# Gated mix of a state-space convolution and a bilinear GLU on one core: first weights split by blocks, inverse sets joined, planner's durations replaced

## The chip, the cores and the metric

The program runs on one core of a Trainium2 chip. Its engines work side by side, each through a list of instructions of its own in a fixed order: TensorE (PE) multiplies matrices, VectorE (DVE) and ScalarE (ACT) do elementwise work, GpSimd (POOL) and SyncE (SP) here mostly issue DMAs. The metric is the device time of one execution in microseconds. Before the change the median of three runs is 632.51 us (631.53 to 634.56).

## The reference

With x = A_u (2048 tokens, 512 channels):

```python
g = sigmoid((x * gate_w).sum(-1, keepdims=True))
a = conv(x, K) + x * D_skip        # K[d,l] = 2 Re sum_n C dt exp(A dt l), N=128, by FFT of length 4096
b = ((B_x @ w_gate) * (B_x @ w_up)) @ w_down      # 512 -> 1792 -> 512
out = g * a + (1 - g) * b
```

All data are float32.

## The kernel before

**The GLU.** The 1792 hidden columns are 14 blocks f of 128, taken in five groups of 3, 2, 3, 3, 3 (`GROUPS`); the tokens are four chunks of 512. One step (`hidden`, 56 in all) is one f for one chunk: 4 gate products into `pg` and 4 up products into `pu`, one for each 128 rows kt of the inputs, then `h` = pg times pu. `down` multiplies h into `y`, 4 products for a step. Each product is three fp32r matmuls: operands are split into a high part (`xhi`, `whi`, `dhi`, `hh`: a ScalarE cast) and a low part (`xlo`, `wlo`, `dlo`, `hl`: a VectorE subtraction). ScalarE scales y into `acc`, which a DMA adds into the output in DRAM; of the last chunk of the last group VectorE sums y into `kt` instead (`ends`).

**The convolution.** For 16 blocks b of 32 channels VectorE and ScalarE build tables of powers (`phases`, `amplitudes`, `direct_powers`, `x_table`, `v_table`) and PE multiplies them into the filter (the set `k<-v,x`, `k_block`). For each quarter q of the channels there follow: the first transform of the filter (`k<-kt,w1k_t`), the second transform of filter and input for T = 0 to 3 (`k<-in,w2s`; of the last quarter `k<-v,w2s` and `k<-x,w2s`), the pointwise product (`m_product`, VectorE), the inverse (`k<-y,w3s`, `m_inverse`), and the last step (`k<-in,w_t` or `k<-v,w_t`, `m_last`), which is scaled by the gate into `ts` and added to the output by DMA. Nearly all these sets write the four PSUM banks `k` and take PE about 1 to 2 us each. The first transform of the input (`u_part`) is eight sets, `k<-in,w_t` too.

**What sets the order.** Each piece of work is a task with an engine, a duration in us, a rank and its inputs (`Work.add`). `Work.run` is a list scheduler: it always takes the task that can start first by its own clock (ties by rank), and writes the instructions of each engine in that order. A task's inputs count as there at the end of their tasks plus a lag (`LAG`); a step's gate and up products may not start before `after` = 10.3 us times the number of the step. On the chip nothing is rescheduled: each engine takes its list in order and waits where an input is late. Before any product PE runs a warm-up (`warm`): products of zeros into a scratch bank.

In the trace all instructions carry line 98 (a helper records them), so they are told apart by their tiles.

Of the kernel before, what the change touches and what calls it, by code (L numbers as in the profile page):

```python
# [45 lines left out]
def fourier_matrices():  # L46
# [17 lines left out]
    for k in range(64):  # L64
# [20 lines left out]
        w4[0], w4[1] = 1.0, (-1.0) ** n1  # L85
    parts = (w1, w1k, w2.reshape(P, 32, 64), w3.reshape(P, 8, 2, 2, 64), w4)
# [56 lines left out]
class Work:  # L143
# [8 lines left out]
    LAG = {"pe": 0.7}  # L152
# [33 lines left out]

    def inputs(self, task):

        lag = self.LAG.get(task.engine, 0.15)
        at = task.after  # L190
        for d in task.deps:
            if d.end is None:
                return None
            at = max(at, d.end + (lag if d.engine != task.engine else 0.0))
        return at

    def slots(self, task, at):

        lag = self.LAG.get(task.engine, 0.15)
        taken = {}  # L200
        for tile in task.tiles:
            if tile.made is not None:
                continue
            n = taken.get(tile.key, 0)
            taken[tile.key] = n + 1
            place = len(tile.had) + n
            if not tile.loose and tile.turn != place:
                return None
            if place >= tile.bufs:
                for d in tile.had[place - tile.bufs].users:  # L210
                    if d.end is None:
                        return None
                    at = max(at, d.end + (lag if d.engine != task.engine else 0.0))
        return at

    def run(self):
# [5 lines left out]
        while any(left.values()):  # L222
# [30 lines left out]
            free[t.engine] = t.end  # L253
# [15 lines left out]
def gated_mix_kernel(  # L269
# [118 lines left out]
    def first_loads():  # L388
# [3 lines left out]
        w0 = load_two(lambda k: ("w", 0, k), in_ev, None, False)  # L392
        x01 = load_two(lambda k: ("x", 0, k), in_y, None, False)
        for t, k, src in ((x01, 0, xsrc(0)), (w0, 0, wts[0][:, :D]), (w0, 1, wts[0][:, D : 2 * D]), (x01, 1, xsrc(1))):
            add("sp", 0.42, lambda t=t, k=k, src=src: sp.dma_start(t.t[:, k], src), w=[(t, k)], dma=256, rank=-1)
        x23 = xT[2 * P : 4 * P, :D].rearrange("(k p) t -> p k t", k=2)
        load_two(lambda k: ("x", 0, 2 + k), in_y, x23)
# [8 lines left out]
        def warm():  # L406
            for _ in range(3):
                pe.matmul(scratch.t, zero.t[:, :P], zero.t, start=True, stop=True)

        add("pe", 4.0, warm, r=[zero], w=[scratch], rank=-1)  # L410

    def weights(fs):
        for f in fs:
            ws[f] = [new("glu", n, [P, 2 * D], F32R, len(GROUPS[0])) for n in ("whi", "wlo")]
            for c in range(2):
                load(("w", f, c), wts[f][:, c * D : (c + 1) * D])
                split(ws[f][0], ws[f][1], c, ("w", f, c))
            if f == 0:
                for kt in range(1, KT):
                    tokens_first(0, kt)  # L420
# [26 lines left out]
    def product(pg, which, w, x, kt, after):  # L447
        base = which * D + kt * P

        def fn():  # L450
            for n, (a, b) in enumerate(THREE):
# [4 lines left out]
        add("pe", 0.69, fn, r=[(w[0], which), (w[1], which), x[0], x[1]], w=[pg], rank=2, after=after)  # L456
# [5 lines left out]
    def hidden(f):  # L462
# [3 lines left out]
        after = T_STEP * len(steps)  # L466
# [5 lines left out]
        for which, kt in pairs:  # L472
            product(pg[which], which, ws[f], x[kt], kt, after)
# [15 lines left out]
    def down(y, r, h, w, first, last):  # L489
# [6 lines left out]
        add("pe", 0.69, fn, r=[*h, *w], w=[y], rank=2)  # L496
# [22 lines left out]
    def ends():  # L519
# [7 lines left out]
        for r, y in ending:  # L527
            t = t0 + r
            add(
                "dve", 0.69,  # L530
# [4 lines left out]
            )  # L535
            add(
                "dve", 0.25,
                lambda r=r: dve.tensor_tensor(
                    out=sums.t[:, r, P * (KT - 1) :], in0=sums.t[:, r, P * (KT - 1) :], in1=late["fin"].t[:, r],
                    op=ALU.add,  # L540
                ),
                r=[late["fin"]], w=[(sums, r)], rank=0.5,
# [40 lines left out]
    def u_part(c):  # L583
# [28 lines left out]
        add("pe", 2.0, fn, r=[ut, m_w1], w=banks[0] + banks[1], rank=1, hold=sts)  # L612
# [130 lines left out]
    def amplitudes(bs):  # L743
# [6 lines left out]
        def exps():  # L750
            for k, l in enumerate(POWERS):
                act.activation(e.t[:, : TB * len(bs), k].rearrange("p (n d) -> p n d", d=TB), rates(), AF.Exp, scale=float(l))

        add("act", 1.3 + NP * (0.13 + 0.0021 * TB * len(bs)), exps, r=[par], w=[e])
# [3 lines left out]
    def phases(b):  # L758
# [12 lines left out]
        def sines():  # L771
            act.activation(rt.t, t.t, AF.Abs)
            act.activation(t.t, t.t, AF.Sin, scale=-TWO_PI)
            act.activation(rt.t, rt.t, AF.Sin, scale=-TWO_PI, bias=half_pi[:, 0:1])

        add("act", 3.6 if b % 2 or not b else 2.3, sines, r=[m_const], w=[t, rt])
# [20 lines left out]
    def leads(b):  # L797
# [4 lines left out]
        add("act", 0.42, lambda: act.copy(x.t[:, :, :, 0], C()), r=[par], w=[(x, ("l", 2))])  # L802
# [58 lines left out]
    def v_table(b):  # L861
# [8 lines left out]
        add("act", 1.3, copies, r=[ri], w=[(v, 2)])  # L870
# [5 lines left out]
        for to, of, n in ((32, 0, 16), (56, 32, 8)):  # L876
# [12 lines left out]
            add("act", 2 * us - 0.2, sq_act, r=src_parts, w=[(v, ("r", k)), sq])  # L889
# [12 lines left out]
    def k_block(b, x, v):  # L902
# [15 lines left out]
        add("pe", 2.07, kgen, r=[x, v], w=[pk], rank=0, hold=[kt])  # L918
# [10 lines left out]
    def k_first(q, kt):  # L929

        tt(0.19, lambda: kt.t[:, 48, :], lambda: kt.t[:, 48, :], lambda: skip[:, q], ALU.add, [m_skip], [kt])
        for h in range(2):
# [17 lines left out]
            add("pe", 2.1, fn, r=[kt, m_w1k], w=banks, rank=-1, hold=sts)  # L950
# [59 lines left out]
    def m_second(q, ins, w):  # L1010
# [18 lines left out]
        add("pe", 2.1, fn, r=[*ins, w], w=banks[0] + banks[1], rank=1, hold=tos)  # L1029
# [40 lines left out]
    def m_inverse(q, T, y, w):  # L1070

        banks, ts = [bank() for _ in range(4)], stage([P, 2, 4, P])

        def fn():
            for i in range(2):
                for k in range(2):
                    for e in range(2):
                        for j in range(4):
                            lanes, cs = slice(32 * j, 32 * j + 32), slice(P * i, P * i + P)
                            pe.matmul(  # L1080
                                banks[j].t[64 * e : 64 * e + 64, cs], w.t[lanes, i, e, k], y.t[lanes, k, e, cs],
                                start=k == 0, stop=k == 1, tile_position=(32 * j, 64 * e),
                            )

        add("pe", 1.15, fn, r=[y, w], w=banks, rank=1, hold=[ts])
        for j in range(4):
            evict(
                q, j, 0.4, lambda j=j: ts.t[:, :, j],
                lambda j=j: banks[j].t[:, : 2 * P].rearrange("p (i d) -> p i d", i=2), [banks[j]], [(ts, j)],
            )  # L1090
        add(
            "sp", 0.42,
            lambda: sp.dma_start(
                y_d[q, 32 * T : 32 * T + 32].rearrange("(j a) n d -> (a n) j d", j=8),
                ts.t.rearrange("p i j d -> p (i j) d"),
            ),
            r=[ts], w=[(m_y, (q, T))], dma=512,
        )


    def m_last(q, half):
# [31 lines left out]
        add("pe", 1.9, fn, r=src, w=banks, rank=1, hold=fins)  # L1133
        for i, f in enumerate(banks):
# [15 lines left out]
            args = ("dve", 0.69, mix_dve) if q == KT - 1 else ("act", 1.2, mix_act)  # L1150
# [13 lines left out]
    def transforms(q):  # L1164
# [11 lines left out]
        now = [loads(0)]  # L1176
        for T in range(4):
# [4 lines left out]
            m_inverse(q, T, m_product(T, k, u2), w3_s)  # L1182
# [88 lines left out]
```

## Time and profile before

| | before |
|---|---|
| median of 3 runs | 632.51 us |
| the profiled execution | 633.44 us |
| its span, first to last instruction | 631.7 us |
| PE busy | 612.6 us, 97% |
| VectorE busy | 495.4 us, 78% |
| ScalarE busy | 399.6 us, 63% |
| GpSimd busy | 106.1 us, 17% |

PE is busy nearly all the time, and the chain of waits that ended last runs over PE for 81% of the span. The first product starts at 7.68 us and the last one at 625.32 us; the span ends 6.3 us after that. VectorE's share falls late: in the page's 40 slices it is busy 5 to 9 tenths up to 520 us, and 1 to 6 tenths behind that.

### The profile page before, as it was taken

To read this page: it belongs to the slowest core of one execution; us is meant where nothing else is said; L and a number is where in the kernel's file an instruction comes from. 1 tells how busy PE (TensorE), PEld (TensorE's weight loads), DVE (VectorE), ACT (ScalarE), POOL (GpSimd) and SP (SyncE) were. 2 spreads that over 40 slices of the span, in tenths; PEclk is the share of its full clock that TensorE was granted. 3 is DMA by queue.
4 is the path that set the end of the run, shared out by engine and by line. 5 is a ranking of instruction groups with operands and counts; after the bars stand their busy time and mean duration, and the time that the engine had idled before them with its cause. 6 is when DMAs were issued, how large, how long until landed. Compare 5 with 4: busy or idle time off the path is not lost.

```text
span 631.7 us, 18000 instructions
## 1 busy us (share of the span) xinstructions
PE 612.6 (97%) x7526; PEld 468.8 (74%) x7526; DVE 495.4 (78%) x764; ACT 399.6 (63%) x931; POOL 106.1 (17%) x157
## 2 busy tenths in 40 slices
PE   8989999999999999999999999999999999998996
PEld 5667677678688887787778778768887887776783
DVE  6958999989969899799778898977998872146524
ACT  4477877885876795668687765785786543333320
POOL 3231523111021021002110202030101011130101
PEclk9999999999999999999999999999999999999998
DMA  8896949559779599578988959597979699897956
GB/s 309 295 335 248 328 136 369 178 159 287 190 183 300 148 242 274 136 217 190 260 196 199 292 159 247 156 190 190 276 165 265 184 255 252 285 248 206 239 129 116
DMA packets 111893, 142.64 MB, mean 226 GB/s; under 512 B 7876, under 2 KB 66756, under 8 KB 111556
## 3 DMA queue, kind: packets, MB, share of 16 engines
q1 hardware_dynamic: 90100, 105.05, 52.7%
q0 software_dynamic: 21568, 36.45, 28.0%
q8 instruction: 59, 0.97, 0.6%
q14 instruction: 22, 0.18, 0.1%
q10 hardware_dynamic: 144, 0.00, 0.0%
HBM read 81.96 MB, written 59.51 MB: 224 GB/s over the span
## 4 chain that ended last, share of the span: by engine, by line
PE 81%; issue 7%; DVE 5%; DMA 4%; POOL 1%; ACT 1%; POOLq 0%
PE y L98 22%; PE pg L98 20%; PE pu L98 20%; PE k L98 19%; DMA x_d<-xhi 2%; DVE x L98 2%; DMA su_d<-ts 1%; DVE v L98 1%; POOL x_d L98 1%; DMA y<-in_xT 1%; DVE m L98 1%; POOL su_d L98 0%; DVE hl L98 0%; DVE wlo L98 0%; DVE ri L98 0%
## 5 line engine op out<-in xcount | busy, mean ns | idle before, releaser
L98 POOL DMA_DIRECT2D out<-acc x60 | 51.5, 916 | 372.2 <-ACT acc L98 341.7
L98 PE MATMUL y<-dhi,hl 128*128 128x512 f32 x224 | 91.4, 408 | 3.8 <-DVE hl L98 3.5
L98 PE MATMUL pg<-xhi,wlo 128*128 128x512 f32 x224 | 90.3, 403 | 3.6 <-ACT h L98 1.5
L98 PE MATMUL pu<-xhi,wlo 128*128 128x512 f32 x224 | 89.7, 400 | 0.6 <-DVE h L98 0.6
L98 PE MATMUL pg<-xlo,whi 128*128 128x512 f32 x224 | 87.6, 391 | 0.1
L98 PE MATMUL y<-dlo,hh 128*128 128x512 f32 x224 | 87.5, 391 | 0.0
L98 PE MATMUL pg<-xhi,whi 128*128 128x512 f32 x224 | 87.5, 390 | 0.0
L98 PE MATMUL y<-dhi,hh 128*128 128x512 f32 x224 | 87.4, 390 | 0.0
L98 PE MATMUL pu<-xlo,whi 128*128 128x512 f32 x224 | 87.4, 390 | 0.0
L98 PE MATMUL pu<-xhi,whi 128*128 128x512 f32 x224 | 87.3, 390 | 0.0
L98 DVE TENSOR_TENSOR h<-pu,h 128x512 f32<-128x512 f32 x56 | 38.6, 689 | 55.9 <-PE pu L98 36.1
L98 ACT ACTIVATE acc<-y,ngate 128x512 f32<-128x512 f32 x76 | 51.5, 686 | 36.5 <-PE y L98 28.9
L98 ACT CAST hh<-h 128x512 fp32r<-128x512 f32 x56 | 34.7, 621 | 57.5 <-DVE h L98 57.5
L98 ACT COPY ts<-k 128x256 f32<-128x256 f32 (+1 forms) x144 | 51.2, 435 | 21.3 <-PE k L98 21.3
L98 PEld LDWEIGHTS y<-dhi,hl 128*128 128x128 f32 x224 | 42.0, 187 | 24.5 <-issue 7.9
L98 PEld LDWEIGHTS pg<-xhi,wlo 128*128 128x128 f32 x224 | 42.0, 187 | 21.0 <-issue 5.0
L98 ACT COPY h<-pg 128x512 f32<-128x512 f32 x56 | 32.9, 588 | 37.7 <-PE pg L98 25.3
L98 PEld LDWEIGHTS pu<-xhi,wlo 128*128 128x128 f32 x224 | 42.0, 188 | 14.8 <-issue 4.7
L98 PEld LDWEIGHTS y<-dhi,hh 128*128 128x128 f32 x224 | 42.1, 188 | 9.3
L98 PEld LDWEIGHTS pg<-xhi,whi 128*128 128x128 f32 x224 | 42.0, 188 | 9.1
L98 PEld LDWEIGHTS pu<-xhi,whi 128*128 128x128 f32 x224 | 42.1, 188 | 9.1
L98 PEld LDWEIGHTS pg<-xlo,whi 128*128 128x128 f32 x224 | 42.1, 188 | 8.6 <-DVE xlo L98 0.5
(105 smaller groups left out, 1128.6 us busy)
## 6 DMA issues: line engine op xcount, KB each, us to landing
out<-acc POOLq DMA_DIRECT2D x60, 256.0 KB, 6.3
xhi<-x_d SPq DMA_DIRECT2D x48, 256.0 KB, 5.1
xlo<-x_d SPq DMA_DIRECT2D x48, 256.0 KB, 5.2
raw<-in_wts SPq DMA_DIRECT2D x36, 256.0 KB, 4.6
su_d<-ts POOLq DMA_DIRECT2D x32, 256.0 KB, 6.2
sk_d<-ts SPq DMA_DIRECT2D x16, 512.0 KB, 5.7
y_d<-ts SPq DMA_DIRECT2D x16, 512.0 KB, 5.0
in<-sk_d SPq DMA_DIRECT2D x12, 512.0 KB, 7.4
```

The source lines that it names most:

```text
L98: got = getattr(self.engine, name)(*args, **kw)
```

## The change

1. The weights of the first block f = 0 are loaded in four pieces of 128 input rows (gate and up columns together, 128 KB each), the first by ScalarE's queue, the others by SP's between the tokens' loads; each piece is split by itself (`first_split`). In f = 0 of the first chunk the product of the two high parts comes first. The warm-up has two products instead of three.
2. `m_inverse` takes two T at once: one set of 64 matmuls instead of two of 32, four evictions of 512 columns instead of eight of 256, and rows of `w4` permuted to fit.
3. In `ends` VectorE adds `fin` before it adds y, so that y's sum is the last operation ahead of the output DMA.
4. The planner: other lags, an overlap between neighbouring tasks on ScalarE and VectorE, other durations; `after` 5 us earlier; the exponentials and the sines are three tasks each instead of one.

```diff
-    LAG = {"pe": 0.7}
+    LAG = {"pe": 0.06, "sp": 0.3, "pool": 0.3}
+    PE_LAG = 0.17
+    OVERLAP = {"act": 0.09, "dve": 0.08}
...
+    def ready(self, task, d):
+        if d.engine == task.engine == "pe":
+            return d.end
+        return d.end + self.LAG.get(task.engine, 0.03) + (self.PE_LAG if d.engine == "pe" else 0.0)
...
-            free[t.engine] = t.end
+            free[t.engine] = t.end - self.OVERLAP.get(t.engine, 0.0)
...
+        for kt in range(KT):
+            t, k, ks = xt[kt // 2], kt % 2, slice(P * kt, P * kt + P)
+            add("sp", 0.42, lambda t=t, k=k, kt=kt: sp.dma_start(t.t[:, k], xsrc(kt)), w=[(t, k)], dma=256, rank=-1)
+            e, q = ("sp", sp) if kt else ("act", act)
+            add(e, 0.42, lambda q=q, ks=ks: q.dma_start(w0.t[:, :, ks], wsrc[:, :, ks]), w=[(w0, ("k", kt))], dma=128, rank=-1)
...
-            for _ in range(3):
+            for _ in range(2):
                 pe.matmul(scratch.t, zero.t[:, :P], zero.t, start=True, stop=True)
...
+    def first_split(kt):
+        hi, lo, t, k = *ws[0], raws["w0"], ("k", kt)
+        cut = lambda x: x.rearrange("p (c d) -> p c d", c=2)[:, :, P * kt : P * kt + P]
+        src = lambda: t.t[:, :, P * kt : P * kt + P]
+        add("act", 0.38, lambda: act.copy(cut(hi.t), src()), r=[(t, k)], w=[(hi, k)], rank=0)
+        add("dve", 0.42, lambda: dve.tensor_tensor(out=cut(lo.t), in0=src(), in1=cut(hi.t).bitcast(F32), op=ALU.subtract),
...
+        three = THREE[::-1] if first else THREE
...
-        add("pe", 0.69, fn, r=[(w[0], which), (w[1], which), x[0], x[1]], w=[pg], rank=2, after=after)
+        add("pe", 0.681, fn, r=[(w[0], part), (w[1], part), x[0], x[1]], w=[pg], rank=2, after=after)
...
-        after = T_STEP * len(steps)
+        after = T_STEP * len(steps) - 5.0
...
-    def m_inverse(q, T, y, w):
-        banks, ts = [bank() for _ in range(4)], stage([P, 2, 4, P])
+    def m_inverse(q, T0, ys, ws):
+        banks, sts = [bank() for _ in range(4)], [stage([P, 2, 2, 2, P]) for _ in range(2)]
         def fn():
+            for t in range(2):
...
-        add("pe", 1.15, fn, r=[y, w], w=banks, rank=1, hold=[ts])
+        add("pe", 2.13, fn, r=[*ys, *ws], w=banks, rank=1, hold=sts)
...
-            m_inverse(q, T, m_product(T, k, u2), w3_s)
+            done.append((m_product(T, k, u2), w3_s))
+            if T % 2:
+                m_inverse(q, T - 1, *zip(*done))
+                done = []
```

**The order that comes of it.** VectorE at the start of the program (`small` is the chain for the time step, `xlo` and `wlo` the low parts of tokens and weights). Before:

```order
L98 TENSOR_SCALAR small<-small 128x4 x3
L98 SCALAR_TENSOR_TENSOR small<-small 128x4 x2
L98 TENSOR_SCALAR small<-small 128x4 x2
L98 TENSOR_TENSOR xlo<-y,xhi 128x512
L98 SCALAR_TENSOR_TENSOR small<-small 128x4 x2
L98 TENSOR_TENSOR wlo<-ev,whi 128x512
L98 SCALAR_TENSOR_TENSOR small<-small 128x4
L98 TENSOR_TENSOR wlo<-ev,whi 128x512
L98 SCALAR_TENSOR_TENSOR small<-small 128x4
L98 TENSOR_TENSOR xlo<-y,xhi 128x512
L98 SCALAR_TENSOR_TENSOR small<-small 128x4 x3
L98 TENSOR_TENSOR xlo<-y,xhi 128x512 x2
```

VectorE at the same place in the changed kernel:

```order
L100 TENSOR_SCALAR small<-small 128x4 x2
L100 TENSOR_TENSOR xlo<-y,xhi 128x512
L100 TENSOR_TENSOR wlo<-ev,whi 128x2x128
L100 TENSOR_SCALAR small<-small 128x4
L100 SCALAR_TENSOR_TENSOR small<-small 128x4 x2
L100 TENSOR_TENSOR xlo<-y,xhi 128x512
L100 TENSOR_TENSOR wlo<-ev,whi 128x2x128
L100 TENSOR_SCALAR small<-small 128x4 x2
L100 SCALAR_TENSOR_TENSOR small<-small 128x4
L100 TENSOR_TENSOR xlo<-y,xhi 128x512
L100 TENSOR_TENSOR wlo<-ev,whi 128x2x128
L100 SCALAR_TENSOR_TENSOR small<-small 128x4 x2
```

Before, both `wlo` of f = 0 stand ahead of the second `xlo`; now there are four half-size ones, one behind each `xlo`. A fourth `xlo` and `wlo` follow directly behind the rows shown.

TensorE around one inverse set (`k<-y,w3s`) between products of the GLU. Before:

```order
L98 MATMUL pu<-xhi,whi 128x512
L98 MATMUL k<-y,w3s 64x128 x32
L98 MATMUL pu<-xhi,wlo 128x512
L98 MATMUL pu<-xlo,whi 128x512
L98 MATMUL pu<-xhi,whi 128x512
```

TensorE around one inverse set in the changed kernel:

```order
L100 MATMUL pg<-xhi,whi 128x512
L100 MATMUL k<-y,w3s 64x128 x64
L100 MATMUL pg<-xhi,wlo 128x512
L100 MATMUL pg<-xlo,whi 128x512
L100 MATMUL pg<-xhi,whi 128x512
```

A set has 64 matmuls instead of 32, and there are 8 sets instead of 16. Counted over the whole list, the convolution's sets stand in 71 separate places between GLU matmuls before (the warm-up counted as one) and in 60 now. Between the first and the last of the sixteen sets `k<-v,x` stand 1428 of the 2016 GLU matmuls before and 1176 now; behind the set `k<-v,w_t`, the last of the convolution, 21 before and 243 now.

VectorE's last rows (`kt` is the sum of the last four row tiles, `ts` the convolution's part of it). Before:

```order
L98 SCALAR_TENSOR_TENSOR kt<-y,ngate,kt 128x512
L98 TENSOR_TENSOR ts<-k,gate 128x512 x3
L98 SCALAR_TENSOR_TENSOR kt<-y,ngate,kt 128x512
L98 TENSOR_TENSOR ts<-k,gate 128x512
L98 TENSOR_TENSOR kt<-kt,ts 128x128 x2
L98 SCALAR_TENSOR_TENSOR kt<-y,ngate,kt 128x512
L98 TENSOR_TENSOR kt<-kt,ts 128x128
L98 SCALAR_TENSOR_TENSOR kt<-y,ngate,kt 128x512
L98 TENSOR_TENSOR kt<-kt,ts 128x128
```

VectorE's last rows in the changed kernel:

```order
L100 TENSOR_TENSOR h<-pu,h 128x512
L100 TENSOR_TENSOR hl<-h,hh 128x512
L100 TENSOR_TENSOR h<-pu,h 128x512
L100 TENSOR_TENSOR hl<-h,hh 128x512
L100 SCALAR_TENSOR_TENSOR kt<-y,ngate,kt 128x512 x4
```

The four `ts<-k,gate` and the four `kt<-kt,ts` now stand together, before the last six pairs of `h` and `hl`, and the four sums over y close the list.

## Rows read from the trace of the kernel before

**Rows 1.** The page's first part: busy us, share of the span, instructions.

```profile
PE 612.6 (97%) x7526; PEld 468.8 (74%) x7526; DVE 495.4 (78%) x764; ACT 399.6 (63%) x931; POOL 106.1 (17%) x157
```

**Rows 2.** Stretches: us, busy of PE, PEld, DVE, ACT, POOL; clock; DMA.

```profile
83.44:520.48 437.04, 432.82 (x5909) 338.36 (x5908) 384.84 (x558) 313.10 (x735) 64.35 (x76) 1.00 0.79 214
62.00:120.00 58.00, 54.91 (x470) 39.58 (x468) 54.80 (x94) 46.02 (x99) 18.10 (x28) 1.00 0.72 254
```

**Rows 3.** PE's waits: who waited <- for whom: us, times, longest.

```profile
PE k L98 <- issue: 3.6, 4, 1.5
PE y L98 <- DVE hl L98: 3.5, 3, 1.5
PE pg L98 <- ACT h L98: 1.5, 2, 1.2
```

**Rows 4.** Timeline, 4 to 14 us: start, us, engine, operation.

```profile
4.96 0.58 DVE L98 TENSOR_SCALAR small<-small 128x4 f32<-128x4 f32 x3 [3.40 <-DMA small<-in_rows]
6.05 0.69 DVE L98 TENSOR_TENSOR xlo<-y,xhi 128x512 fp32r<-128x512 f32 x1
...
9.36 1.30 DVE L98 TENSOR_TENSOR xlo<-y,xhi 128x512 fp32r<-128x512 f32 x2
12.36 0.39 PE L98 MATMUL pg<-xhi,whi 128*128 128x512 f32 x1
12.89 0.58 ACT L98 COPY h<-pg 128x512 f32<-128x512 f32 x1
13.52 0.50 PE L98 MATMUL pg<-xhi,wlo 128*128 128x512 f32 x1
```

**Rows 5.** Groups by form: operation, count, busy us, mean ns, idle before.

```profile
L98 PEld LDWEIGHTS pg<-xhi,whi 128*128 128x128 f32 x224 | 42.0, 188 | 9.1
L98 PEld LDWEIGHTS k<-acc 128*128 128x128 f32 x6 | 1.9, 330 | 3.5 <-issue 2.1 <-DVE acc L98 1.5
```

**Rows 6.** Timeline of PE around one inverse set.

```profile
598.16 0.39 PE L98 MATMUL pg<-xlo,whi 128*128 128x512 f32 x1
598.39 0.39 PE L98 MATMUL pg<-xhi,whi 128*128 128x512 f32 x1
598.71 1.21 PE L98 MATMUL k<-y,w3s 32*64 32x128 f32 x64
599.85 0.50 PE L98 MATMUL pu<-xhi,wlo 128*128 128x512 f32 x1
600.18 0.40 PE L98 MATMUL pu<-xlo,whi 128*128 128x512 f32 x1
```

**Rows 7.** Timeline of PE: two halves of one set, back to back.

```profile
567.62 1.16 PE L98 MATMUL k<-v,w2s 64*32 64x128 f32 x64
568.51 1.16 PE L98 MATMUL k<-x,w2s 64*32 64x128 f32 x64
569.60 0.50 PE L98 MATMUL pu<-xhi,wlo 128*128 128x512 f32 x1
```

**Rows 8.** Groups by form, VectorE's two for a step, ScalarE's table loads.

```profile
L98 DVE TENSOR_TENSOR h<-pu,h 128x512 f32<-128x512 f32 x56 | 38.6, 689 | 55.9 <-PE pu L98 36.1 <-issue 16.7 <-ACT h L98 1.9
L98 DVE TENSOR_TENSOR hl<-h,hh 128x512 fp32r<-128x512 f32 x56 | 38.4, 685 | 8.6 <-ACT hh L98 8.6
L98 ACT ACT_TABLE_LOAD x20 | 25.7, 1283 | 2.8 <-DMA pb<-par_d 1.3 <-PEq L1260 1.2
```

**Rows 9.** Timeline of the end, PE and VectorE.

```profile
625.32 0.39 PE L98 MATMUL y<-dhi,hh 128*128 128x512 f32 x1
625.75 0.75 DVE L98 SCALAR_TENSOR_TENSOR kt<-y,ngate,kt 128x512 f32<-128x512 f32 x1 [0.96 <-PE y L98]
626.53 0.29 DVE L98 TENSOR_TENSOR kt<-kt,ts 128x128 f32<-128x128 f32 x1
```

**Rows 10.** DMA issues: queue, count, KB each, median us to landing.

```profile
out<-kt SPq DMA_DIRECT2D x4, 256.0 KB, 4.9
pb<-par_d SPq DMA_DIRECT2D x2, 32.0 KB, 2.7
```

More of the change, by code (lines that the diff above doesn't have):

```diff
@@ L212, in slots @@
                         return None
-                    at = max(at, d.end + (lag if d.engine != task.engine else 0.0))
+                    at = max(at, self.ready(task, d))
         return at
@@ L414, in weights @@
             ws[f] = [new("glu", n, [P, 2 * D], F32R, len(GROUPS[0])) for n in ("whi", "wlo")]
+            if f == 0:
+                for kt in range(KT):
+                    first_split(kt)
+                    if kt + 1 < KT:
+                        tokens_first(0, kt + 1)
+                continue
             for c in range(2):
@@ L445, in gated_mix_kernel, with product @@
     THREE = ((1, 0), (0, 1), (0, 0))
-    def product(pg, which, w, x, kt, after):
+    def product(pg, which, w, x, kt, after, first):
         base = which * D + kt * P
+        part = ("k", kt) if first else which
+        three = THREE[::-1] if first else THREE
         def fn():
-            for n, (a, b) in enumerate(THREE):
+            for n, (a, b) in enumerate(three):
                 pe.matmul(
@@ L472, in hidden @@
         for which, kt in pairs:
-            product(pg[which], which, ws[f], x[kt], kt, after)
+            product(pg[which], which, ws[f], x[kt], kt, after, not steps[1:] and f == 0)
         h = new("glu", "h", [P, D])
@@ L529, in ends @@
             add(
+                "dve", 0.25,
+                lambda r=r: dve.tensor_tensor(
+                    out=sums.t[:, r, P * (KT - 1) :], in0=sums.t[:, r, P * (KT - 1) :], in1=late["fin"].t[:, r],
+                    op=ALU.add,
+                ),
+                r=[late["fin"]], w=[(sums, r)], rank=0,
+            )
+            add(
                 "dve", 0.69,
@@ L534, in ends @@
                 r=[y, (m_gate, LAST)], w=[(sums, r)], rank=0,
[L535 to L542, printed above, removed]
             )
@@ L1101, in m_last @@
+        for h in range(2):
+            st = sts[h]
+            b0 = 32 * (T0 + h)
+            add(
+                "sp", 0.42,
+                lambda b0=b0, st=st: sp.dma_start(
+                    y_d[q, b0 : b0 + 32].rearrange("(u a) n d -> (a n) u d", u=8),
+                    st.t.rearrange("p t i j d -> p (t i j) d"),
+                ),
+                r=[st], w=[(m_y, (q, T0 + h))], dma=512,
+            )
     def m_last(q, half):
@@ L1174, in loads @@
             )
-        now = [loads(0)]
+        now, done = [loads(0)], []
         for T in range(4):
```

101 lines of the change are left out of this document (50 added, 51 removed).

## The prediction

> **What bounds the kernel now.** I read the page's busy shares first: PE 97%, VectorE 78%, ScalarE 63% [rows 1]. So PE's own list sets the time, and an edit counts by what it takes from PE's list, from PE's waits, or from the two ends where PE stands idle. Then the stretches: from the first table set `k<-v,x` (83.44 us) to the last (520.48 us) PE is busy 432.82 of 437.04 us, and VectorE 384.84 us [rows 2]. PE's waits for a named releaser are few: 3.5 us for `hl`, 1.5 us for the copy of `pg`, and 3.6 us of stops inside sets that have no releaser [rows 3]. Last the two ends: step 1 begins at 13.52 us [rows 4], and the last product starts at 625.32 us, 6.3 us before the span's end of 631.7 [rows 9].
>
> A GLU matmul takes 0.23 us from start to start (598.16 to 598.39, rows 6); over many, 0.227.
>
> **Joined inverse sets: -3.0 us.** A set runs from 598.71 to 599.85, 1.14 us. Going in costs 0.32 - 0.23 = 0.09 us, coming out 0.33 - 0.23 = 0.10 us [rows 6]. Two sets apart take 2 x 1.33 = 2.66 us. How long 64 matmuls take in one set no row shows for this shape. The nearest is the second transform, of which the first half takes 0.89 us up to the second's start and the second half 1.09 us up to the next product [rows 7]: a half that is followed by its like is shorter than one that is followed by something else. So a joined set takes 1.14 + 0.89 = 2.03 us at best, 2.28 us at worst, and 0.19 us around it. A pair saves 0.19 to 0.44 us, eight pairs 1.5 to 3.5 us. I take 3.0, near the row. The evictions fall from eight of 256 columns to four of 512 and lie on ScalarE, which is 63% busy. The joined set waits for the later of two products; the GLU matmuls behind it in PE's list would wait with it. That is inside the term for waits below. The writes to `y_d` stay sixteen of 512 KB, each half now up to one product later.
>
> **Fewer places between the products: -0.4 us.** The sets stand in 60 places instead of 71. Eight of the eleven come from the joining and are counted; the other three save at most 3 x 0.19 = 0.6 us and at least nothing.
>
> **The start: -0.4 us, from -1.5 to +2.6.** Before, `pg` of f = 0 gets its last product at 12.36 us, ScalarE copies it at 12.89, and the next step starts at 13.52, 1.16 us after that product [rows 4]. In the new order the high product is first, but the second and the third of each kt need `xlo` and `wlo`, so VectorE sets the pace. Its list up to the last `wlo` of f = 0 has four `xlo`, four half-size `wlo` and eight `small`. Before, four `xlo`, two whole `wlo` and seven `small` took from 6.05 to 9.36 + 1.30 = 10.66 us, 4.61 us [rows 4]. With 0.4 us for a half (an estimate between half of the 0.685 us of the same subtraction, rows 8, and the whole) and 0.1 for one more `small`, that is 4.9 us. The first `xlo` stands behind two `small`; their 2 KB are now issued second on ScalarE's queue, some 0.4 us later, so 4.96 + 0.4 + 0.4 = 5.8 us. The last low part is there at 10.7 us instead of feeding a product at 12.36; step 1 starts at 11.9 to 12.1: 1.5 us earlier at best. The same 1.5 MB are loaded as before, in smaller pieces; no row shows weights loaded so, and if a piece lands late the end of the range below covers it.
>
> [...]
>
> **The end: -0.7 us, from -2.5 to +0.3.** Behind the last product come a sum of 0.75 us, the addition of `ts` of 0.29 us [rows 9] and the output DMA. The addition now stands earlier: -0.29 us. The output DMAs took 4.9 us to land, in the company of GpSimd's last two additions of `ts` into the output; the smallest landing of the trace is 2.7 us for 32 KB [rows 10]. The last set of the convolution now has 243 GLU matmuls behind it instead of 21, 55 us instead of 5, so this company is gone: between 0 and -2.2 us, and I take -0.7. Against it: with two `y` buffers the third row tile's product waits for the first one's sum. From the start of a last product to its sum's end it takes 0.43 + 0.75 = 1.18 us [rows 9], and only four matmuls, 0.91 us, are there to cover it: +0.27. All of the last products stand behind that wait.
>
> **The planner: 0 us, from -5 to +20.** This moves nearly every row and adds no PE work. What it removes can be the waits for `hl` and `pg` [rows 3]. What it adds is pressure on VectorE. Between the first and the last `k<-v,x` there are 252 GLU matmuls fewer, 57.2 us, and by the order one second transform and one last set fewer (2 x 2.2 us by rows 7) and five joined inverse sets (5 x 2.28) for twelve (12 x 1.33): 9.0 us. So PE needs 437.0 - 57.2 - 9.0 = 370.8 us there, with its old waits. VectorE does 25 instructions fewer there (529 for 554), 23 of them on 128 x 512 at 0.687 us [rows 8]: it needs 384.8 - 15.8 = 369.0 us. That is a share of 99.5% where it had 88%; its best long stretch before was 54.80 of 58 us, 94.5% [rows 2]. What hides VectorE's waits before, its slack, is gone. In return the last 164 us are nearly free of it. I take 0: the waits that better durations remove against those that a full VectorE brings back.
>
> Two more table loads on ScalarE (22 for 20, 1.28 us each, rows 8) come from the split exponentials and sines; ScalarE's idle third hides them, and uncovered they cost 2.6 us. The read of the sums into `kt` now stands ahead of the last 14 loads of tokens on SP's queue; the first of them is needed over 100 matmuls, some 25 us, later, so I cost it at nothing. The host's permutation of `w4` costs nothing.
>
> **Sum.** -3.0 - 0.4 - 0.4 - 0.7 + 0 = -4.5 us. The profiled execution took 633.44 us, 0.93 more than the median of the runs: 633.4 - 4.5 = 628.9, as a median 628.0 us.
>
> **Rivals.** (A) VectorE becomes the bound of the table stretch. For it: 99.5%. Against: instructions interleaved by true durations leave fewer holes than the old order did. If it stays at 94.5%, its 369.0 us take 390.5, 19.7 more than PE's 370.8; 633.4 - 4.5 + 19.7 - 0.9 = 647.7 us. It decides from VectorE's waits of some 9 us in the stretch on: 1.8 are free, 4.5 eat the gains. (B) The planner also takes out PE's waits for `hl` and `pg`, 5.0 us: 623.0 us. For it: these are exactly waits that wrong lags make. Against: VectorE's fullness. [...] (D) The change doesn't give what it says: the joined sets wait for their second half and PE loses what it saved, leaving the ends: 631.4 us.
>
> **How the numbers follow.** My forecast, 628.0 with its own range of 624 to 632, has a chance of 0.37; A 0.21, B 0.20, C 0.12, D 0.10. About 0.5%, 3.2 us, can be told from no change. Faster by more (below 629.3): three quarters of mine, all of B, a little of C and D, 0.51. Slower by more (above 635.7): nearly all of A, 0.20. The rest, 0.29, is no change. The range goes to the better end of B, 619, and into A as far as 641, leaving out A's upper half.
>
> **What would show it.** Sets `k<-y,w3s` of 128 records (the trace counts two for each matmul of the order) and 2.0 to 2.3 us, eight of them. [...] From the last product to the span's end 5.4 us. Between the first and last `k<-v,x` about 371 us; 380 and more, with PE's waits for VectorE grown, is A. I am wrong if PE's waits for VectorE and ScalarE together pass 10 us, or fall under 1.

## The result, and the profile after

The changed kernel takes 637.13 us (median of 20 runs, 633.19 to 643.60) beside 633.75 us for the kernel before on the same chip: ratio 1.0044, 95% interval 1.0023 to 1.0066. It is slower by 0.4%; 628.0 was forecast. The profiled execution took 638.18 us, its span 636.4.

The page's busy shares and the clock in 40 slices, against [rows 1]:

```profile
PE 611.7 (96%) x7524; PEld 471.3 (74%) x7524; DVE 485.0 (76%) x762; ACT 399.2 (63%) x907; POOL 106.2 (17%) x157
...
PEclk9989999999999999999999999998989999999999
```

PE is busy for as long as before in a longer span, so the loss shows as waits, and three slices show the clock at 8 tenths. TensorE's waits, against [rows 3] (who waited <- for whom: us in all, times, longest; `issue` stands for a stop without a releaser, in which TensorE waits for nothing that the profile names):

```profile
PE k L100 <- issue: 8.8, 4, 3.3
PE y L100 <- ACT acc L100: 3.1, 1, 3.1
PE pu L100 <- issue: 1.6, 2, 1.5
PE k L100 <- DVE acc L100: 1.5, 1, 1.5
PE y L100 <- DVE dlo L100: 1.3, 1, 1.3
```

Stops without a releaser went from 4.8 to 10.4 us; a wait of 3.1 us for ScalarE is new; those for `hl` are gone. Over the whole list, stops included, the waits grew from 12.8 to 20.3 us.

The wanted parts did come. TensorE's start, a joined set, and the last product with its sum on VectorE (start, us, engine, operation), against [rows 4], [rows 6] and [rows 9]:

```profile
5.38 0.68 PE L100 MATMUL pg<-xhi,whi 128*128 128x512 f32 x1
6.75 0.50 PE L100 MATMUL pg<-xlo,whi 128*128 128x512 f32 x1 [0.69 <-DVE xlo L100]
...
12.46 0.50 PE L100 MATMUL pg<-xhi,wlo 128*128 128x512 f32 x1
...
540.00 2.09 PE L100 MATMUL k<-y,w3s 32*64 32x128 f32 x128
542.02 0.50 PE L100 MATMUL pu<-xhi,wlo 128*128 128x512 f32 x1
...
631.99 0.39 PE L100 MATMUL y<-dhi,hh 128*128 128x512 f32 x1
632.41 0.75 DVE L100 SCALAR_TENSOR_TENSOR kt<-y,ngate,kt 128x512 f32<-128x512 f32 x1 [1.29 <-PE y L100]
```

The first product starts at 5.38 instead of 7.68 us, step 1 at 12.46 instead of 13.52, a joined set takes 2.02 us for two of 1.14, and 4.4 us instead of 6.3 lie behind the last product's start.

Where the time went shows in two places. First TensorE, then ScalarE, near 33 us:

```profile
33.37 0.39 PE L100 MATMUL pu<-xhi,whi 128*128 128x512 f32 x1
36.90 0.79 PE L100 MATMUL y<-dhi,hl 128*128 128x512 f32 x1 [3.15 <-ACT acc L100]
```

```profile
32.77 0.21 ACT L100 ACTIVATE score<-score 128x4 f32<-128x4 f32 x1 [2.14 <-DVE y L100]
35.65 0.62 ACT L100 CAST xhi<-raw 128x512 fp32r<-128x512 f32 x1 [2.67 <-DMA raw<-in_xT]
36.17 1.26 ACT L100 ACTIVATE acc<-y,ngate 128x512 f32<-128x512 f32 x2
```

The cast of the next chunk's tokens stands ahead of the eviction `acc` in ScalarE's list and waits for its load; the eviction, and with it the next `y`, wait behind it. The second place is a table set 6 GLU matmuls behind a second transform:

```profile
424.46 2.06 PE L100 MATMUL k<-in,w2s 64*32 64x128 f32 x128
...
428.04 1.53 PE L100 MATMUL k<-v,x 128*32 128x64 f32 x84
432.34 1.45 PE L100 MATMUL k<-v,x 128*32 128x64 f32 x44 [2.78 <-issue]
433.73 0.79 PE L100 MATMUL y<-dhi,hl 128*128 128x512 f32 x1
```

The set stops after 84 of its 128 records, waits for nothing the profile names, and ends at 433.73 instead of some 430.0. The same happens at 463 us (3.7 us lost) and 519 us (2.7 us), also 6 matmuls behind another set. Stretches of it (us; busy of PE, PEld, DVE, ACT, POOL; granted clock; DMA share and GB/s):

```profile
36.52:39.93 3.41, 3.03 (x8) 1.99 (x9) 1.93 (x3) 3.23 (x17) 2.17 (x4) 0.50 1.03 416
429.00:432.40 3.40, 0.62 (x39) 0.46 (x30) 3.37 (x8) 0.79 (x2) 1.19 (x2) 1.00 1.16 291
432.47:435.88 3.41, 3.41 (x49) 2.86 (x47) 3.33 (x6) 1.99 (x5) 0.00 (x0) 0.50 1.13 262
```

Around the end of each of the three longest standstills (33, 429, 465 us), from 0.4 us before it to 1.6 us behind it, a stretch of 3.41 us begins in which the granted clock is 0.50: at most 1.7 us lost each (an estimate, half of 3.41). The account, with the waits counted from the first product on (10.7 us before, 18.8 now): 8.1 us more of waits + up to 5.1 us of clock - 2.3 (start) - 1.9 (end) - 3.6 (eight pairs of sets, 0.26 us in the set and 0.19 around it) = up to +5.4 us; the span grew by 4.7.

### The profile page after: what moved, and what is told of

It reads as the page before. It is cut to its first block, busy times and chain, and to the rows that moved or that the text cites. A ratio compares the mean times of both kernels' runs of the same rounds, so it can differ in the third digit from the quotient of the medians.

```text
span 636.4 us, 17971 instructions
## 1 busy us (share of the span) xinstructions
PE 611.7 (96%) x7524; PEld 471.3 (74%) x7524; DVE 485.0 (76%) x762; ACT 399.2 (63%) x907; POOL 106.2 (17%) x157
## 4 chain that ended last, share of the span: by engine, by line
PE 79%; DVE 9%; ACT 4%; DMA 4%; issue 4%; ACTq 0%; DVEq 0%
PE y L100 22%; PE pu L100 20%; PE pg L100 20%; PE k L100 18%; DVE x L100 2%; DMA dt_d<-small 2%; DVE v L100 1%; ACT L100 1%; DVE t L100 1%; DVE wlo L100 1%; DMA raw<-in_xT 1%; DMA small<-in_rows 1%; DVE ri L100 1%; ACT rt L100 1%; DVE hl L100 1%
## 5 line engine op out<-in xcount | busy, mean ns | idle before, releaser
L100 PE MATMUL y<-dlo,hh 128*128 128x512 f32 x224 | 88.8, 396 | 1.3 <-DVE dlo L100 1.3
L100 PE MATMUL y<-dhi,hh 128*128 128x512 f32 x224 | 88.8, 396 | 0.0
L100 ACT COPY ts<-k 128x512 f32<-128x512 f32 (+1 forms) x116 | 48.7, 499 | 23.1 <-PE k L100 23.1
L100 PEld LDWEIGHTS pg<-xhi,whi 128*128 128x128 f32 x224 | 42.2, 188 | 10.7 <-ACT whi L100 1.7
L100 PEld LDWEIGHTS y<-dlo,hh 128*128 128x128 f32 x224 | 42.9, 192 | 9.7 <-DVE dlo L100 1.6
L100 PEld LDWEIGHTS pu<-xlo,whi 128*128 128x128 f32 x224 | 42.1, 188 | 9.8 <-issue 1.8
```

What stands on the lines that cost most here:

```text
L100: got = getattr(self.engine, name)(*args, **kw)
```

## The experiments

**One half of the change at a time.** `old_planner` has edits 1 to 3 with the old planner:

```diff
-    LAG = {"pe": 0.06, "sp": 0.3, "pool": 0.3}
+    LAG = {"pe": 0.7}
...
-        after = T_STEP * len(steps) - 5.0
+        after = T_STEP * len(steps)
```

> The changed kernel with the planner's numbers of before (lags, durations, no overlap, steps 5 us later, exponentials and sines one task each again); the split first weights, the joined inverse sets and the reordered last sums stay. Theory (the loss comes from the order that the new numbers give): the three other edits are left with what the trace of the changed kernel gave them, start -2.3 us, inverse sets -3.5, end -1.9, so 633.8 - 7.7 = 626 us (623 to 629), with no stretch at the lower clock and no stop of TensorE over 2 us. Rival 1 (the split weights delay the chain for the time step and so ScalarE's list at 33 us, whatever the planner's numbers): the 3.1 us wait of the y products and its 1.7 us of lower clock stay, about 631 us. Rival 2 (sets of 128 matmuls in one piece starve TensorE's instruction supply, whatever stands around them): stops as in the changed kernel, about 634 us.

Measured: 633.80 us, ratio to before 0.9988 (0.9962 to 1.0014). The theory's 626 was wrong. First product at 5.46 us, sets and end as in the changed kernel, so the 7.7 us were had. Against them stand this order's own waits (19.6 us in all, 12.8 before) and three stretches of 3.41 us at a granted clock of 0.50, where the theory had no such stretch and no stop over 2 us. The traced execution took 637.57 us, 3.8 more than the median, so in most executions they cost less:

```profile
PE k L100 <- issue: 5.5, 4, 1.9
PE pg L100 <- ACT h L100: 3.4, 3, 2.3
PE pg L100 <- DVE xlo L100: 2.3, 1, 2.3
```

`planner_only` is the kernel before with edit 4 alone, the reverse of the diff above.

> The kernel before with the planner's numbers of the changed kernel and none of its three other edits (first weights, inverse sets and last sums as before). Theory (the numbers let sets of 128 matmuls and halves of 64 stand 6 GLU matmuls apart, where the old lag kept 9): stops behind the two v,x at a distance of 6 (about 3 us each) and shorter ones behind the halves, with ScalarE's order at 33 us as in the changed kernel or not (the start is late, so the gate is there in time): 636 to 642 us. Rival 1 (the numbers cost nothing by themselves; the loss of the changed kernel comes with the split first weights): 632 to 635 us. Rival 2 (the numbers are as good as they were meant to be): 628 to 632 us.

Measured: 641.64 us, ratio 1.0103 (1.0075 to 1.0131), at the theory's upper end. Its first wait, against 3.6 us in [rows 3], and one of its sets, again 6 matmuls behind another:

```profile
PE k L98 <- issue: 10.1, 9, 2.3
```

```profile
333.70 0.68 PE L98 MATMUL k<-v,x 128*32 128x64 f32 x31
336.69 1.62 PE L98 MATMUL k<-v,x 128*32 128x64 f32 x97 [2.31 <-issue]
```

The planner's numbers alone cost 1.0%; the other edits alone gain nothing that can be told; together 0.4% is lost.

`old_start` is the changed kernel without edit 1.

```diff
-        w0 = raws["w0"] = in_ev([P, 2, D])
+        w0 = load_two(lambda k: ("w", 0, k), in_ev, None, False)
...
-        three = THREE[::-1] if first else THREE
+        three = THREE
```

> The changed kernel with the first weights loaded and split as before, the old order of the three products in f = 0 and three warm-up products; the planner's numbers, the joined inverse sets and the last sums stay as changed. Theory (the wait at 33 us comes from an earlier start that the gate and the tokens' loads do not follow, so the start's 2.3 us are given back there): first product at 7.6 us, the wait of the y products for ScalarE's acc under 1.5 us and no lower clock there; stops at the four places where v,x stands 6 GLU matmuls behind another set (3 us each where both have 128): 636 to 641 us. Rival (the wait at 33 us is the planner's order alone): the wait of 3.1 us for acc stays and the late start adds 2.3 us, 640 to 644 us.

Measured: 635.31 us, ratio 1.0000 (0.9971 to 1.0029), just under the expected range. First product at 7.47 us, no wait for `acc` over 1 us. Starting 2.1 us earlier thus gains nothing: with the early start PE stands at 33 us until the tokens and the gate are there. The later sets stand in another order too, but their stops without a releaser come to nearly the same, 10.3 us for 10.4.

**The early wait.** `acc_first` changes ScalarE's list alone (`behind` moves one task of the finished order, and what depends on it, behind another):

```diff
+        self.behind(order, named["cast", ("x", 1, 1)], named["acc", 0, 1])
```

> The changed kernel with one difference: in ScalarE's list the cast of the second chunk's tokens kt = 1 (xhi) stands behind the evictions of row tiles 0 and 1 (acc) instead of ahead of them; what needs the cast follows it. Theory: the wait of the y products at 33 us (3.1 us on acc) goes and with it the stretch at the lower clock behind it (1.7 us): 637.1 - 4.8 = 632.3 us (630.5 to 634.5). Rival 1 (the next task needs the same late load of tokens, so PE waits for xhi a little later instead): the wait moves to the pg products of the second chunk, 635.5 to 637.5 us. Rival 2 (PE is not what paces this stretch; VectorE's list does): no change in the end of the table stretch, 636.5 to 637.5.

Measured: 635.49 us, ratio 1.0029 (1.0001 to 1.0058); the interval overlaps that of the changed kernel, so the gain of 1.6 us is not told from noise. In the trace part of the theory holds: the wait falls from 3.1 to 1.8 us, the stretch at 0.50 from 36.52 us on is gone, and the three stops at the sets stay to 0.05 us as they were. But now `acc` waits for the gate, the second limit on the early start:

```profile
32.30 0.21 ACT L100 ACTIVATE score<-score 128x4 f32<-128x4 f32 x1 [1.87 <-DVE y L100]
34.32 1.27 ACT L100 ACTIVATE acc<-y,ngate 128x512 f32<-128x512 f32 x2 [1.81 <-DVE ngate L100]
```

**The distance between sets.** `sets_apart` and `sets_joined` move sets of the changed kernel in the finished order, nothing else (the edits in short):

```diff
+        for x in sets:                      # sets_apart: until 15 GLU matmuls stand before x
+            self.behind(order, x, product_that_makes_15)
...
+        for x, y in zip(sets, sets[1:]):    # sets_joined: where at most 9 stand between
+            self.behind(order, x, last_product_before_y)
```

> The changed kernel with one difference: every set of 128 matmul instructions (k<-v,x, k<-in,w2s, k<-v,w2s with k<-x,w2s, k<-y,w3s) that stood fewer than 15 GLU matmuls behind the set before it is moved back until 15 stand between (9 of 40 sets move, by 3 to 9 matmuls, 0.7 to 2 us); its consumers follow it. Theory (a set takes TensorE's instructions faster than they are fetched, and a second set soon behind it meets an empty supply): the stops of 3.69, 3.66 and 2.65 us at 428, 463 and 519 us go, with two stretches at the lower clock of 1.7 us each: 637.1 - 13.4 = 623.7 us at best, 624 to 629 with what the delayed consumers cost. Rival 1 (the stops come by chance, from the DMA traffic alone, wherever sets stand): the stops are elsewhere, 634 to 639 us. Rival 2 (removed stops come back as waits for VectorE, which is full in that stretch): the sets v,x end as late as before, 635 to 637.5.

Measured: 631.89 us, ratio 0.9972 (0.9945 to 0.9998), against 1.0044 for the changed kernel. The stops without a releaser shrink and do not vanish (5.2 us for 10.4), so the time stays above the 624 to 629 expected. The same set as at 428 us above, now 15 matmuls behind the other, loses 1.1 us instead of 3.7:

```profile
431.53 1.37 PE L100 MATMUL k<-v,x 128*32 128x64 f32 x78
433.76 0.97 PE L100 MATMUL k<-v,x 128*32 128x64 f32 x50 [0.86 <-issue]
```

> The changed kernel with one difference, the opposite of the one before: at the places where two sets of 128 matmul instructions have at most 9 GLU matmuls between them (7 places) the first is moved back until it touches the second. Theory (instruction supply): every one of the 7 pairs now ends in a stop of 3 to 4 us (three do in the changed kernel), and most of them in a stretch at the lower clock: 4 x 3.7 + 4 x 1.7 = 21 us at most, 645 to 660 us. Rival 1 (stops by chance or by DMA traffic alone): 634 to 640 us. Rival 2 (what counts is the number of places where the stream of products is broken): 7 places fewer at 0.19 us each, 635.8 us.

Measured: 646.06 us, ratio 1.0190 (1.0153 to 1.0226). The trace is of the shortest of its six executions, 642.41 us. In it all seven pairs lose 1.2 to 3.5 us (the theory had 3 to 4), in the second set or, once, just behind it, 17.7 us together; in the changed kernel three of them do, 10.0 us. Of the 17.7, 2.3 us are waits for a bank that ScalarE has yet to empty, which theory and rivals had left out. A pair that ran undisturbed at a distance of 9, now touching:

```profile
228.93 2.06 PE L100 MATMUL k<-v,x 128*32 128x64 f32 x128
...
232.14 1.65 PE L100 MATMUL k<-y,w3s 32*64 32x128 f32 x92 [0.78 <-ACT kt L100]
235.76 0.69 PE L100 MATMUL k<-y,w3s 32*64 32x128 f32 x30 [1.98 <-issue]
```

Chance alone is out: the stops come and go with the distance. But the distance is not all: in the changed kernel the set at 261.56 us also stands 6 matmuls behind another and loses nothing. What decides stands under "What is short".

`both_mends` joins `acc_first` and `sets_apart`.

> The two mends in one kernel: ScalarE's acc evictions of row tiles 0 and 1 ahead of the late xhi cast, and at least 15 GLU matmuls between sets of 128. Theory (two causes that do not touch each other): the gains add, -1.6 us and -5.2 us as measured apart against 637.1, so 630.3 us (628.5 to 632), with no stretch at the lower clock inside the run. Rival (PE is given back its wait elsewhere: what the sets lose reappears as waits for VectorE once the start is earlier): 631.5 to 633.5 us.

Measured: 630.11 us, ratio 0.9942 (0.9911 to 0.9973), as expected to 0.2 us. That fits two causes that add; it does not show it, since the gain of `acc_first` alone is not told from noise and the rival's 631.5 us lies within the interval. One stretch at a granted clock of 0.50 is left (47.53 us), where the theory had none.

`apart_27` asks for 27 instead of 15.

> As both mends, with at least 27 GLU matmuls between sets of 128 instead of 15. Theory (the supply needs time to refill): the stops left at a distance of 15 (1.13, 1.96, 0.94 and 1.65 us at 431, 462, 515 and 525 us) go, -4 to -6 us against both mends, 624.5 to 627 us. Rival 1 (15 is enough, and what is left comes by chance): 630 us, stops of the same sum elsewhere. Rival 2 (the later sets hold up VectorE's products and the loads behind them): over 631 us, with waits of the sets k<-y,w3s or k<-in,w_t for VectorE or DMA over 1 us.

Measured: 657.12 us, ratio 1.0353 (1.0310 to 1.0396): rival 2, and far worse than it said, though by another sign: the sets themselves waited 0.7 us for a load, 3.2 for ScalarE and not at all for VectorE. The stops without a releaser did fall, to 1.7 us (5.4 in `both_mends`). One of VectorE's waits (5.0 us of this kind in the changed kernel) and the first of PE's:

```profile
DVE y L100 <- ACT ev L100: 28.5, 8, 8.6
```

```profile
PE y L100 <- DVE hl L100: 10.5, 6, 4.5
```

VectorE's list stood as planned for earlier sets and waited in order for their evictions; in the table stretch of the changed kernel it is busy 96% of the time and has little to give, and PE then waited for `hl`.

`before_apart` is the kernel before, its order kept, with the distance of 15.

> The kernel before, its order kept, with the mend of the sets alone: at least 15 GLU matmuls between sets of 128 (and halves of 64); sets that stood 9 apart move by 6, some by more where moves add up. Theory (9 is already better than 6, so there is less to win): the stops of 0.99, 0.90 and 1.81 us at 248, 374 and 582 us shrink, 633.8 - 2.5 = 631.3 us (630 to 633). Rival 1 (before had no such stops, its losses come by chance): 633 to 635 us. Rival 2 (sets moved late hold up VectorE, as at a distance of 27): over 635 us, with VectorE's waits for ScalarE's ev or kt grown by several us.

Measured: 633.57 us, ratio 0.9983 (0.9963 to 1.0003): inconclusive. The three named stops are gone, but all stops without a releaser still sum to 4.0 us (4.8 before), at other sets, and other waits grew (for `wlo` from 0.7 to 1.8 us, for `acc` from 0.2 to 1.7).

**What is short.** `sets_twice` and `wide_added` add work to the same eight sets (the edits in short; `PLACES` are their b):

```diff
-            for d in range(TB):
+            for d in [*range(TB)] * (2 if b in PLACES else 1):       # sets_twice
...
+            for _ in range(4 if b in PLACES else 0):                 # wide_added
+                pe.matmul(pk.t, x128, v512, start=True, stop=True)
```

> The changed kernel, with eight of the sets k<-v,x (b = 0, 1, 2, 3, 4, 8, 12, 13, all at least 42 GLU matmuls behind the set before) multiplied twice in place, the second time over the first with the same numbers: 256 matmul instructions and 256 weight loads in one piece. Theory (instruction supply): besides 8 x 2.0 us of work each piece stops for 2 to 3.5 us near its middle, as adjoining sets did: +16 and +16 to +28, so 669 to 682 us. Rival (stops come from DMA traffic or chance, not from the number of instructions): +16 to +18, 653 to 656 us.

> The control of the kernel before: the same eight sets have four matmuls of 128x512 (float32, multiplied in two passes each, eight instructions) ahead of them in the same bank, overwritten by the set: about the same time of PE (4 x 0.47 = 1.9 us by the set k<-in,w_t of the same shape) with 16 instead of 256 instructions more. Theory: +15 us of work and no new stops, 651 to 654 us. Rival (any longer occupation of PE away from the products brings the stops and the waits): as sets_twice.

Measured: 686.85 us (ratio 1.0819) and 670.25 us (1.0569), both above what the theory expected. One place of each, `sets_twice` first:

```profile
112.46 3.38 PE L100 MATMUL k<-v,x 128*32 128x64 f32 x223
119.98 1.11 PE L100 MATMUL k<-v,x 128*32 128x64 f32 x33 [4.14 <-issue]
```

```profile
111.54 5.70 PE L100 MATMUL k<-v,x 128*128 128x512 f32 x136
```

All eight pieces of 256 stop, for 1.0 to 4.6 us, 25 us together; besides, the granted clock is 0.50 for 30.7 us, against 10.2 in the changed kernel. In the control a place takes 3.5 us more (I had priced it at 1.9: its four matmuls over 128 rows, 8 of the 136 records, took 0.88 us each) with at most 0.1 us of stop, though PE is longer away from the products; of the other 5 us of its +33 the trace shows 1.3 as waits elsewhere. In these two it is instructions that run out, not time. The page's instruction queue (q8: packets, MB) says the same, for the changed kernel (`wide_added` has the same line) and for `sets_twice`:

```profile
q8 instruction: 59, 0.97, 0.6%
q8 instruction: 67, 1.10, 0.7%
```

The eight pieces have 2048 instructions more (1024 matmuls, 1024 weight loads), and with them came 8 packets and 0.13 MB more: a packet of 16 KB for 256 instructions, exactly one set. In the changed kernel all 59 packets have 16,384 bytes and come while the program runs, from 30.3 to 618.8 us.

The traces hold when each packet came, and that settles the cause. Count TensorE's instructions (matmuls, weight loads and the few others that the trace has for it) in the order of their start, from 0. In the sixteen kernels traced here there are 85 stops without a releaser over 0.4 us, and all 85 end at an instruction whose number leaves 193 or 194 when divided by 256: the stop of 2.78 us above ends at number 10689, which is 41 x 256 + 193. So in these kernels TensorE stopped where one packet's instructions end and the next one's begin. Each of the 85 ends 1.1 to 1.7 us after a packet has landed (that one at 432.34 us, its packet at 430.86), and at none of the 942 such borders does TensorE go on sooner than that.

A packet landed between 4.9 us before and 6.6 us after TensorE began the 256 instructions ahead of those that it brought, 2.6 us after in the median. What decided here was therefore how long TensorE took for these 256, stops left out: under 4 us, 55 of 151 ended in a stop; 4 to 6 us, 27 of 176; over 6 us, 3 of 615. A short distance between sets made this time short, but a single set did it too: before the change the set at 313.46 us, 120 GLU matmuls behind the one before it, stopped for 0.99 us.

`late_pieces` puts three such pieces behind the convolution, 60, 40 and 20 products before the last (in short):

```diff
+    for n in range(3):
+        add("pe", 4.2, piece_of_256, r=[late["y"]], w=[bank()], rank=3).name = ("probe", n)
```

> The changed kernel with three more pieces of 256 matmul instructions of the shape of k<-v,x (as in the kernel with eight sets twice, but over tiles that are there anyway, into a bank that nothing reads), 60, 40 and 20 products of three matmuls before the last product: about 590, 608 and 626 us, of which the second and third lie where the profile of the changed kernel shows the DMA engines at 4 tenths or less. Theory (the fetch of TensorE's instructions comes late only behind other transfers): the first piece stops for 1 to 4.5 us as the eight did, the second and third for under 0.5 us; +12.6 us of work and 1 to 5 us, 651 to 655 us. Rival (the fetch itself is slower than 256 such matmuls, whatever the DMA does): all three stop for 2 to 4 us, +19 to +25 us, 656 to 662 us.

Measured: 658.23 us (ratio 1.0381). The three pieces, and the stretches around them:

```profile
593.18 3.85 PE L100 MATMUL k<-v 128*32 128x64 f32 x256
...
599.25 0.40 PE L100 MATMUL pu<-xlo,whi 128*128 128x512 f32 x1 [1.79 <-issue]
...
612.73 3.09 PE L100 MATMUL k<-v 128*32 128x64 f32 x197
618.41 1.63 PE L100 MATMUL k<-v 128*32 128x64 f32 x59 [2.59 <-issue]
...
634.86 3.85 PE L100 MATMUL k<-v 128*32 128x64 f32 x256
```

```profile
585.00:600.00 15.00, 13.21 (x298) 11.11 (x297) 1.39 (x2) 2.38 (x4) 2.58 (x3) 1.00 0.52 72
605.00:620.00 15.00, 12.41 (x292) 10.47 (x290) 1.38 (x2) 1.99 (x3) 1.72 (x2) 0.96 0.57 143
622.00:640.00 18.00, 18.00 (x319) 15.14 (x318) 2.77 (x4) 3.45 (x6) 1.70 (x2) 0.99 0.24 31
```

By its time this is the rival's range; by the pieces it looks like the theory: where the DMA engines are busy for 0.52 and 0.57 of the stretch a piece stops for 1.8 and 2.6 us, at 0.24 not at all. The time is more than the theory's since the granted clock was 0.50 for 20.5 us instead of 10.2. And the pieces show less than they seem to. The second did not land in quiet time as I had meant. The third was spared by its place: its last instructions share a block of 256 with products, which takes 4.0 us in all, and the next packet lands 2.3 us after the block's start; with a block as short as those that ended in the other two stops (2.4 and 2.1 us) it would have stopped for about 1 us (an estimate from these times). What the sixteen traces show is that packets came later where the DMA engines were busier: in the median 1.9 us after the start of the block where the DMA share of the 6 us around it is under 0.3, 3.6 us where it is 0.9 and more. Why a packet starts when it does no run here shows.

**The distance as a rule of the planner.** `planned_apart` (5.4 us) and `planned_15` (3.4 us) let the planner keep it, so the other engines' lists follow:

```diff
+                if t.name and t.engine == "pe":
+                    start = max(start, apart)
...
+            if t.name and t.engine == "pe":
+                apart = t.end + 5.4
```

> The changed kernel with acc ahead of the late cast and the distance made a rule of the planner: a set of 128 may not start until 5.4 us after the set before it ended (24 GLU matmuls); unlike the kernel with 27, VectorE's and ScalarE's lists are planned anew with it. Theory (27 failed since VectorE's list stood as planned for earlier sets, and waited in order for ScalarE's evictions): with the lists planned for it VectorE's waits for ev and kt stay under 10 us in all, the stops at the sets fall under 4 us in all, 626 to 631 us. Rival 1 (VectorE has no slack left for any delay of the sets, planned or not): the last v,x ends 10 us or more later, 636 to 645 us. Rival 2 (a distance of 24 brings no fewer stops than 15): 630 to 633 us.

Measured: 632.22 us, ratio 0.9951 (0.9925 to 0.9976), a little over the range and within rival 2's; stops at sets fell to 2.5 us, but VectorE's waits for `ev` are 20.8 us, not under 10.

> The changed kernel with acc ahead of the late cast and the distance as a rule of the planner, 3.4 us (15 GLU matmuls) instead of 5.4 us. Theory (most of the gain is had from 6 to 15, and planning anew costs as little as moving by hand): 628 to 632 us, as both mends (630.1) and the rule of 5.4 us (632.2). Rival 1 (a new order brings new waits of its own by chance): 633 to 638 us, with a wait over 2 us at a place where the other two have none.

Measured: 626.75 us, ratio 0.9893 (0.9861 to 0.9925), better than expected and faster than both kernels: 1.1% under before. It is one order, and how much of its gain comes from the distance and how much from waits that this order happens not to have, no run separates. Its waits sum to 11.1 us; the stops without a releaser are 2.1 of them:

```profile
PE pg L100 <- ACT xhi L100: 1.8, 1, 1.8
PE y L100 <- ACT acc L100: 1.7, 1, 1.7
...
PE pu L100 <- issue: 1.2, 1, 1.2
...
PE k L100 <- issue: 0.9, 2, 0.6
```

## Why the prediction was wrong

**Joined sets (-3.0): right.** 2.02 us for a set, at the lower end; about -3.6.

**Start (-0.4): size wrong, and paid back.** VectorE set the pace as said (last `wlo` of f = 0 ready at 10.96, 10.7 forecast), step 1 started at 12.46, 1.06 us earlier than before, where I had 11.9 to 12.1 and then took 0.4; the first product came 2.3 us earlier. Left out was what needs the start's second half: the gate and the next chunk's tokens came no earlier, so PE waited at 33 us. `old_start` shows the net gain as none. No run shows the +2.6 us at the worse end of the range, for which C's 0.12 stood, nor the -0.4 set between the two ends: only the first product took 0.68 us, and from 7.42 us on the others took 0.23 from start to start, at a granted clock of 1.00 up to 20 us. In `apart_27`, `planned_apart` and `planned_15`, with the same start, the granted clock was 0.50 for 3.41 us from about 8 us on: at most 1.7 us lost (an estimate, half of 3.41).

**End (-0.7): right in direction, too small.** -1.9 us. I had put the gain on the convolution's earlier end; `old_planner`, with only 18 GLU matmuls behind it, has the same 4.4 us there, so it comes without that. From VectorE's last end to the span's end it is 4.8 us before and 3.3 in both of these; why the last DMA lands sooner no run shows.

**Planner (0, from -5 to +20): the step that failed.** By itself it cost 1.0% (`planner_only`). I let it add pressure on VectorE alone and set that against the waits for `hl` and `pg`. The one for `hl` did go, the one for `pg`'s copy fell from 1.5 to 1.0 us, and the table stretch was as long as forecast:

```profile
87.38:457.79 370.41, 366.77 (x5394) 288.15 (x5393) 356.31 (x528) 286.69 (x669) 54.34 (x65) 1.00 0.83 225
```

370.4 us for 371: rival A fell. VectorE is busy for 356.3 us there, 96%, where I had worked out a need of 369.0 us, 99.5%; so my sum put it 13 us too near its bound. But my term left out what the new numbers do to PE's own order. The old ones, with their lag of 0.7 us, kept sets at least 9 GLU matmuls apart; with the new ones, whose lag is 0.06, some stand 6 apart, and a set took its 256 instructions, one packet, in 2.0 us. The trace of before had that in view: the 3.6 us of stops "inside sets that have no releaser" were read and given no mechanism; three of the four stood in sets 9 matmuls behind another. That the lag alone sets the distance no run shows: lags, durations and overlaps were changed together. Added by it: 5.6 us of stops and two stretches at a granted clock of 0.50. The rest is the wait at 33 us with a third. The sign that I had named, PE's waits for VectorE and ScalarE passing 10 us, did not show (9.9 us, just under); it left out the stops without a releaser.

**Rivals B and D.** B's waits for `hl` went, and others came. D's joined sets waited for no engine (one, at 519 us, stopped for 2.3 us without a releaser); the kernel still lost what it saved, elsewhere.

## What to carry to other kernels

Where one engine is busy 97% of the time, an edit of a planner is not free even if it moves no work: the five orders of this kernel whose waits I summed carried 11 to 20 us of them, more than all wanted edits together. Read the stops without a releaser before an edit and ask at which instruction each ends: here every one ended where a packet of 256 instructions did. So count how long the engine takes for 256 instructions in a row, and put longer ones between runs of many short ones: here 55 of 151 such blocks under 4 us ended in a stop, and 3 of 615 over 6 us. A rule of the planner did that better than moving the finished list: 632.2 us against 657.1 at the wide distance, 626.8 against 630.1 at 15 matmuls, where the intervals overlap. And ask of an early start whether what the next phase needs comes earlier too: here 2.1 us of it gained nothing.

## What the runs showed of the hardware

- TensorE's instructions came in packets of 16 KB, 256 at a time, while the program ran. All 85 stops without a releaser over 0.4 us ended at the border of two packets, 1.1 to 1.7 us after the landing of the second.
- Over twelve of these kernels (without `sets_joined` and the three with added work), of 20 places where a set begins 1.5 us (6 GLU matmuls) behind another, 12 lost over 0.5 us against the shortest set of their kind, 1.4 us on average over the 20; at 2.2 us (9), 9 of 29; at 2.9 to 3.2 us, 5 of 12; at 3.5 to 5.3 us, 18 of 119; farther off, 20 of 312 (0.08 us on average).
- Around the end of the three longest standstills of the changed kernel (2.8 to 3.3 us in one piece) the granted clock fell to 0.50 for 3.41 us. The trace of `sets_joined`, whose pairs stopped for at most 2.4 us in one piece, shows no such stretch at any of the seven; but its mean granted clock was 0.997, and in the five other executions 0.987 to 0.992, and in `planner_only` a stop of 2.06 us (230.56 us) has one. So which standstills are followed by it is not shown.
- The stops were nearly the same in another kernel that shares most of the order: 3.69, 3.66 and 2.65 us at the three sets in the changed kernel, 3.73, 3.67 and 2.66 in `acc_first`.
